# Attention and gated FFT convolution on one core: turns of q, k and x as two 64-row products, and the global keys at the end of each key tile

## The chip, the core and the metric

The kernel runs on one NeuronCore of a Trainium2 chip. The metric is the device time of one execution in microseconds (us); the median of several runs counts, and single runs of this kernel differ by some tenths of a per cent. A profile is one execution taken by the hardware profiler; its span is a little shorter than the device time. Engine names in the profile: PE is TensorE's products, PEld its weight loads, DVE is VectorE, ACT is ScalarE, POOL is GpSimd, SP is SyncE, which here only starts transfers. L711 is line 711 of the kernel.

## The reference

Causal attention with a window of 96 keys, 8 global keys and a linear bias by distance (4 batches, 8 heads, 768 positions, 64 per head), then a gated convolution over the sequence done by FFT.

```python
scores = scale * np.matmul(q, k.transpose(0, 1, 3, 2))
is_global = pos[None, :] < int(n_global)                 # 8
is_local = (rel >= 0) & (rel < int(n_local))             # 96
dist = np.where(is_global & ~is_local, float(n_local), np.abs(rel))
scores = scores - slopes[:, None, None] * dist           # kept keys only
a = softmax(scores);  x = (a @ v), heads side by side     # (4, 768, 512)
proj = x @ w_proj;  x1, x2, x3 = three parts of 512
x2_conv = irfft(rfft(x2) * rfft(filter_fft))              # length 768
out = (x1 * x2_conv * x3) @ w_out
```

## The kernel before, in words

**One list of operations, one order.** `graph()` creates some thousand operations (an operation is a few instructions on one engine), each with what it reads and writes. The string `ORDER` at the top lists their numbers, in the order in which they were created, as `357P0`: number, engine (P TensorE, V VectorE, A ScalarE, G POOL, S SP) and, for TensorE, the PSUM banks that it takes. Each engine runs its operations in that order; an instruction that waits holds up all that stand behind it on its engine. `i17b0` is 17 products on zeros at the start. The costs beside the operations served to find the order and have no effect on the chip.

**Attention** (`attention`, once per batch, in three column groups `GRP` of 2, 2 and 3 key tiles). Keys are cut into 7 tiles of 112 (`KL`); the last one starts at 656, so that it also holds 112. A tile of keys has 128 rows: rows 0 to 7 hold the 8 global keys, rows 8 to 15 zeros, rows 16 to 127 the 112 keys. Each stage:

- Loads. POOL starts one transfer per tile of q, k and v (`load_q`, `load_rows`, `load_run`). The global rows of v are copied inside SBUF by SP (`load_global`) for batches 1 to 3. In batch 0 they come by a transfer of their own into X (`first_rows`), and VectorE spreads them over the tiles. VectorE zeroes the 16 free rows of kn (named kz).
- Turns. `turned` (L661) turns q and k to put the head dimension on the partitions: per tile four 128x128 transposes as products with a unit matrix (L668), into one bank, for one tile or two; then one copy per bank by VectorE or ScalarE into QT or KT (helper line L306). For the first four tiles, `turned32` does it from float32. In groups 1 and 2 of batch 3, `crossed` has SP transpose by DMA instead. `global_keys` copies the global columns into all tiles of KT.
- Scores. `scores`: two heads side by side, each a product of 64 rows (L711), in two banks. In batch 0 the bias is added there by products (L698); in later batches exp(bias) is multiplied in afterwards. ScalarE takes the exp (L739), VectorE multiplies with the mask (L751).
- Values (`values`): 65-column products (L769, L774), a reciprocal (L799) and a scaling into xn (L793). They read the v tiles and their global rows.
- `transpose_x` (L804): turns xn into xT as `turned` does (L815), with one copy per bank.
- `gate`: products of 384 columns with parts of w (L860), x1, x3 and their product.

**Convolution** (`conv`): the sequence is folded (`butterfly`), projected (L934), transformed (L622), multiplied with the filter's transform, transformed back (L959, L962), joined, gated and projected (L986), then stored.

**Set-up.** `distances` builds the bias tables dg, near, edge and far on POOL and VectorE; `masks` takes their exp and `spread` completes it; `tables` makes the sine tables, for which ScalarE has to load another function table than for exp. The operation `warm` on ScalarE takes an exp of one number to have a table loaded early.

The change touches `ORDER`, `load_rows`, `load_first32`, `load_v`, `load_global`, `setup`, `distances`, `masks`, `turned32`, `global_keys`, `crossed`, `turned`, `scores`, `transpose_x`, `first_tiles`, `load_first` and `first_rows`; in `butterfly`, `gate` and `crossed_x` only the names of what is read and written.

Of the kernel before, what the change touches and what calls it, by code (L numbers as in the profile page):

```python
# [16 lines left out]
P = 128  # L17
NG = 8
KL = 112
LO = P - KL  # L20
HUGE = 1.0e5
# [19 lines left out]
4V 0S 1A 2S 3A 30V 9G 32A 31A 14V 13V 11V 10A 33V 22G 34V 23V 60A 62A 12V 27V 5V 65A 36G 39G 19S 35A 15V 25V 24G 63A  # L41
16V 40G 18V 42G 41G 59A 45G 28V 8V 26V 46G 48G 29A 47G i17b0 74P0 75V 61A 70P1 72P2 71V 68P3 69V 84P45 64A 106P0 76P1
37G 58A 92P67 73A 79A 78A 93P 88P23 77V 94P 85P 38G 108P1 89P 49G 86P 107A 66V 90P 95A 44G 43G 109V 112P0 113V 87A
110P1 111V 80P67 81P 82P 20V 91A 51G 67V 120P01 83A 114P45 121A 152P2 153V 50G 154P3 155V 118P67 158P0 115A 159V 119A
156P2 157V 17V 116P45 21V 117A 160P67 161A 162P23 163A 96P45 97V 98V 101P01 166P67 167A 164P45 122P23 52G 102V 103V
123V 127P01 104P6 124V 128V 53G 129V 7G 217P7 165A 105A 99P4 168P23 125P6 130P5 258G 100V 218A 126A 212P4 131A 173P01
137P5 132P6 169V 170V 171P2 213A 219V 220V 221A 174V 175V 176P7 138P3 259G 172A 357P0 214V 215V 133P2 134A 267G 266G
216A 224P6 177V 199V 198V 206V 139V 385P7 184P4 358A 55G 135V 255G 189P5 140A 141V 386V 179P7 225A 257G 355P3 256G
264G 226A 183P0 265G 359A 6A 353P1 191A 201V 143P5 227V 181A 136V 194P7 56G 57G 185A 200V 202V 356V 383P0 228V 229A
205V 260G 186A 354V 208V 230A 223V 361P23 145A 203V 196A 367P45 362A 364P67 384V 178P1 207V 148P0 365A 295P2 204V 360V  # L50
368A 180V 396P45 150A 296A 397A 390P67 209V 210V 211V 187V 363V 370P01 371A 391A 293P3 294A 270G 369V 291P2 280P0 366V
387P67 222V 292A 398V 388A 231V 232V 233V 234V 393P45 299P3 300A 394A 54G 281A 282P2 283A 429P1 273G 306P3 307A 278P6
279A 147P7 149A 286P2 372V 261S 235V 236V 272G 287A 389V 142P3 433P6 434A 271G 431P7 144A 263G 430A 485G 237V 373P45
262S 151V 268G 297P2 298A 240P6 484G 241A 182V 193P3 195A 374V 432V 238P2 239A 392V 243P6 244A 269G 375V 395V 378P01
486G 379V 380V 435P45 436A 487G 197V 438P23 439A 404P67 405V 146V 376P0 496G 406V 245P1 246A 377V 437V 581P4 284P5
285A 444P23 445A 441P67 442A 407P1 188P0 488G 582V 399P45 381P2 408A 440V 585P3 274G 190V 400V 401V 446V 583P0 382A
586V 252P67 254A 253A 275G 276G 495G 584V 402P1 403A 447P45 489G 490S 443V 613P7 614A 248P23 448V 494G 587A 249A 304P6
305A 452P01 410P7 250A 412A 500G 247V 712G 449V 450P2 453V 454V 425P6 451A 251V 501G 455P3 659P7 456V 502G 427A 493G
302V 660A 595P01 589P45 498G 478V 590A 596A 592P23 593A 588A 414P6 458P7 499G 727G 468P4 416A 301V 661P5 308V 711G
460A 303V 242V 729G 594V 409P0 657P1 658V 611P2 309V 288V 612A 289V 424P6 426A 428V 477V 479V 290V 411A 470A 662A  # L60
473P1 475A 420P7 422A 415P6 413V 312P4 480V 313A 320P5 725G 417A 324P1 472P0 321V 474A 669P23 325A 598P67 599A 523P4
481V 714G 510P1 670A 316P5 314P0 192V 511A 600V 672P23 621P67 317V 524A 715G 482V 812P1 315A 591V 673A 322P4 323A 622A
310P0 311A 813V 730G 814A 418V 419P5 318P1 319A 597V 506P4 507A 421V 491S 463P5 465A 624P67 618P01 619A 666P23 457P4
667A 519P5 674V 625A 483V 508P0 663P23 881S 615P67 713G 326V 327V 328V 329V 623V 330V 520A 664A 462P1 423V 509A 620V
720G 728G 497G 616A 521P5 492G 606P23 505G 333V 334V 464A 467P0 469A 522A 607V 601P67 466V 277G 602V 608V 459A 626V
350P1 810P5 514P0 665V 351A 716G 347P4 603A 503G 835S 671V 525P1 526A 348A 476V 344P2 717S 722G 811V 837S 504G 527P5
345A 515A 528A 617V 668V 632P67 331V 604P4 605A 678P23 532P0 633V 634V 533A 679V 512P5 513A 680V 332V 808P1 627P67
628V 882S 534P0 675P45 676V 609P2 809A 629V 535A 610A 635P1 335P3 677V 630P2 631V 529V 636A 721G 836S 471V 336A 724G
530V 883S 821P01 822A 818P67 819A 820V 815P45 816A 726G 880S 723G 838S 516V 338P3 839V 652P2 654A 681S 339A 642P6 644A
817V 648P7 531V 846P45 517V 682S 840P23 683S 650A 847A 518V 823V 824P01 825A 826V 647P6 841A 643P7 645A 638P4 640A  # L70
719G 827P01 828V 884V 341P5 829V 342A 649A 646V 653P7 849P01 850A 536V 732G 537V 461V 651V 705V 891P45 343S 892A
888P23 704V 851V 637P6 544P0 689P1 707V 639A 655A 545A 548P4 731G 691A 549A 550P6 542P5 893V 842V 540P7 543A 706V 352S
538P0 539A 552P1 553A 695P4 551A 641V 700P0 541A 702A 708V 697A 690P1 830P67 546P0 692A 848V 685P4 684P1 831V 832V
889A 687A 843P23 693V 890V 709V 885P67 340S 547A 844A 894P45 733P0 895A 886A 554V 710V 896V 718S 750P2 855P45 856V
# [1174 lines left out]
```

## Time and profile before

| | us |
|---|---|
| three runs | 170.34, 170.29, 169.12 |
| median | 170.29 |
| profiled execution, device time | 168.69 |
| its span | 166.8 |
| busy: PE, DVE, ACT, POOL | 160.3, 152.9, 144.9, 73.6 |
| first product of work (L635) to the first gate (L860) | 7.52 to 25.56 |
| last product ends | 160.7 |

The page's second part shows the span in 40 slices, a digit is a busy share in tenths:

```profile
PE   7999999999999999999999989999999999999990
DVE  5898979999999999999999979999999999999950
ACT  4589979999999998999999998999896788696731
DMA  5999999999999999999999990804052104300685
```

Three engines are busy nearly throughout, and the DMA engines up to 95 us. "Busy" counts an instruction from its start to its modelled end, and consecutive instructions overlap, so a row's mean duration is longer than the distance at which such instructions follow each other. That distance is read from start times.

### The profile page before, as it was taken

Reading aid. Unit: us, or ns where it says so; the run is one execution under the profiler, and the core shown is the slowest. Engines: PE = TensorE matmul, PEld = TensorE weight load, DVE = VectorE, ACT = ScalarE, POOL = GpSimd, SP = SyncE. Lnnn points to the kernel's source line nnn. Section 1 sums busy time; section 2 is a strip of 40 time slices with the busy share of each in tenths; the row PEclk is TensorE's granted clock in tenths of the full one; section 3 lists DMA queues with packets and bytes.
Section 4 is the critical chain, followed back from the end, with each engine's and each line's share of the span. In section 5 each row is a group of like instructions: output and inputs, shape, how many; then the busy total and the mean of one; then the engine's idle time right before and its main releaser. Section 6 shows DMA issues by size and latency. Waiting matters only on the chain.

```text
span 166.8 us, 4251 instructions
## 1 busy us (share of the span) xinstructions
PE 160.3 (96%) x1621; PEld 99.8 (60%) x1621; DVE 152.9 (92%) x336; ACT 144.9 (87%) x302; POOL 73.6 (44%) x99
## 2 busy tenths in 40 slices
PE   7999999999999999999999989999999999999990
PEld 2566787664567876666457746765744844575430
DVE  5898979999999999999999979999999999999950
ACT  4589979999999998999999998999896788696731
POOL 7999999973889934999570000000000000000000
PEclk9999999999999999999999999999999999999999
DMA  5999999999999999999999990804052104300685
GB/s 121 193 141 127 130 171 166 169 208 181 169 164 154 155 150 63 92 140 149 158 157 130 125 130 19 265 5 118 17 132 51 63 4 181 137 0 0 246 317 194
DMA packets 92916, 22.06 MB, mean 132 GB/s; under 512 B 85760, under 2 KB 89824, under 8 KB 92896
## 3 DMA queue, kind: packets, MB, share of 16 engines
q0 software_dynamic: 75952, 11.95, 100.9%
q1 hardware_dynamic: 14864, 9.33, 23.9%
q10 hardware_dynamic: 2080, 0.52, 1.7%
q8 instruction: 12, 0.20, 0.5%
q14 instruction: 8, 0.07, 0.1%
HBM read 24.94 MB, written 6.29 MB: 187 GB/s over the span
## 4 chain that ended last, share of the span: by engine, by line
PE 58%; DVE 33%; issue 4%; DMA 3%; ACT 0%; DVEq 0%; SPq 0%
PE bank L860 15%; PE bank L986 9%; DVE E L751 8%; PE bank L934 6%; PE bank L959 4%; PE bank L302 4%; DVE xn L793 4%; PE bank L698 3%; DMA KT<-kn 3%; PE bank L711 3%; PE bank L668 3%; PE bank L622 3%; PE bank L769 2%; DVE g L871 2%; PE bank L774 2%
## 5 line engine op out<-in xcount | busy, mean ns | idle before, releaser
L860 PE MATMUL bank<-xT,w 128*128 128x384 f16 x256 | 47.9, 326 | 0.0
L739 ACT ACTIVATE E<-bank 128x832 f16<-128x832 f32 (+2 forms) x64 | 42.8, 759 | 1.1 <-PE bank L711 1.0
L860 PEld LDWEIGHTS <-w 128*128 128x128 f16 x256 | 23.6, 98 | 15.4 <-issue 0.7
L322 POOL DMA_DIRECT2D kn<-in_k_dram x27 | 22.5, 848 | 6.7 <-PE bank L668 4.8
L322 POOL DMA_DIRECT2D vn<-in_v_dram x28 | 24.0, 865 | 2.2 <-DMA w<-in_moe_w_proj_dram 0.9
L986 PE MATMUL bank<-wo,y 128*128 128x512 f16 x96 | 22.9, 379 | 0.1
L751 DVE TENSOR_TENSOR E<-E,mask 128x832 f16<-128x832 f16 (+1 forms) x36 | 21.7, 622 | 0.0
L322 POOL DMA_DIRECT2D qn<-in_q_dram x21 | 18.8, 904 | 3.5 <-PE bank L934 3.2
L310 ACT ACTIVATE ot<-bank 128x512 f32<-128x512 f32 x22 | 12.8, 615 | 5.9 <-PE bank L986 3.8
L793 DVE TENSOR_TENSOR xn<-bank,rc 128x512 f16<-128x512 f32 (+1 forms) x22 | 16.8, 766 | 0.6 <-DVE rc L799 0.2
L310 ACT ACTIVATE ab<-bank 128x512 f16<-128x512 f32 x24 | 14.6, 655 | 1.2 <-PE bank L934 1.2
L869 ACT CAST g<-bank 128x384 f16<-128x384 f32 x30 | 14.5, 523 | 1.2 <-PE bank L860 1.2
L769 PEld LDWEIGHTS <-E 128*128 128x128 f16 x224 | 14.0, 97 | 2.3 <-issue 0.4
L769 PE MATMUL bank<-vn,E 128*128 128x65 f16 x224 | 15.3, 193 | 0.0
L310 ACT ACTIVATE x<-bank 128x384 f16<-128x384 f32 x26 | 13.5, 528 | 2.0 <-PE bank L860 1.3
L986 PEld LDWEIGHTS <-y 128*128 128x128 f16 x96 | 9.1, 98 | 10.1 <-DVE y L1066 0.2
L774 PE MATMUL bank<-vn,E 128*128 128x65 f16 x192 | 15.1, 193 | 0.0
L711 PE MATMUL bank<-QT,KT 64*128 64x208 f16 (+1 forms) x224 | 14.0, 244 | 0.9 <-DVE KT L306 0.7
L306 ACT CAST X<-bank 128x512 f16<-128x512 f32 x24 | 14.2, 643 | 0.3 <-PE bank L622 0.2
L306 ACT CAST eo<-bank 128x384 f16<-128x384 f32 x29 | 13.4, 542 | 0.3 <-PE bank L962 0.3
L774 PEld LDWEIGHTS <-E 128*128 128x128 f16 x192 | 13.2, 97 | 0.5
L711 PEld LDWEIGHTS <-KT 64*128 64x128 f16 x224 | 8.7, 94 | 6.4 <-issue 2.5
(148 smaller groups left out, 337.4 us busy)
## 6 DMA issues: line engine op xcount, KB each, us to landing
out_dram<-ot SPq DMA_DIRECT2D x24, 256.0 KB, 2.4
vn<-in_v_dram POOLq DMA_DIRECT2D x28, 112.0 KB, 5.4
kn<-in_k_dram POOLq DMA_DIRECT2D x27, 112.0 KB, 5.2
qn<-in_q_dram POOLq DMA_DIRECT2D x21, 128.0 KB, 5.6
w<-in_moe_w_proj_dram POOLq DMA_DIRECT2D x4, 256.0 KB, 5.7
g<-in_moe_filter_fft_dram POOLq DMA_DIRECT2D x1, 768.0 KB, 10.2
ot<-in_q_dram ACTq DMA_DIRECT2D x2, 256.0 KB, 6.6
w<-in_moe_w_proj_dram POOLq DMA_DIRECT2D x1, 512.0 KB, 7.2
```

The lines of the kernel that those rows point to most:

```text
L306: {"A": nc.scalar.copy, "V": nc.vector.tensor_copy, "G": nc.gpsimd.tensor_copy}[e](out, in_)
L310: self.nc.scalar.mul(out, in_, c)
L322: return self.g.op(eng, 0.57 + 0.00035 * nbytes[0] if eng == "G" else 0.5, lambda _: e.dma_start(dst, src), w=w, r=r, nbytes=nbytes, name= ...
L711: nc.tensor.matmul(bs[hh].f32()[:, off:off + w], self.KT[hs, hp, P * m:P * m + P], self.QT[hs, hp, KL * m:KL * m + w], start=(off == 0 and ...
L739: nc.scalar.activation(dst, src(), Act.Exp, scale=self.scale)
L751: g.op("V", dve(w, 2), lambda _: nc.vector.tensor_mul(eo, eo, mk), r=[("mask", 2 * hp), ("mask", 2 * hp + 1)], w=[("E", hp, gi)], name="ma ...
L769: nc.tensor.matmul(o[:, n, hh], ef[:, at:at + P], vt[:, t, 2 * hp + hh, 0:D + 1], start=first, stop=(t == 0), skip_group_check=True)
L774: nc.tensor.matmul(o[:, n, hh], ef[:, at:at + P], vt[:, t - 1, 2 * hp + hh, 0:D + 1], start=False, stop=True, skip_group_check=True)
L793: nc.vector.tensor_mul(to, o[:, :, :, 0:D].rearrange("p i (t h) d -> p i t h d", h=2), rc.rearrange("p i (t h) o -> p i t h o", h=2).to_br ...
L860: nc.tensor.matmul(bk.f32()[:, 0:h], self.w[:, c, o + P * j:o + P * j + P], self.xT[:, c, h * s:h * s + h], start=(c == 0), stop=(c == 3))
L869: first = g.op("AV", {"A": act(h), "V": 0.0005}, lambda e: nc.scalar.copy(x3, pts[1].f32()[:, 0:h]) if e == "A" else None, use=[pts[1]], w ...
L986: nc.tensor.matmul(bk.f32(), y[:, c, P * t:P * t + P], self.wo[:, c, :], start=(c == 0), stop=(c == 3))
```

## The change

The key tile's rows are moved: the keys stand in rows 0 to 111 (the last tile now starts at 672 and holds 96), the global keys in rows 112 to 119, and the rest is zero in KT. kn needs no zeroed rows. Every turn becomes two products: rows 0 to 63, and rows 64 to the end, on the two halves of the array, each 64 columns or less, into two banks; each bank is copied out by an operation of its own (in group 2 of `transpose_x` by two instructions). In batch 0 the global rows of v come by `load_global` as in the other batches. The tables of `distances` are built for the new rows, with instructions on rows 96 to 127 that change the rows from 112 on. `warm` takes a sine. `ORDER` is new as a whole (1,060 entries instead of 1,018), with 13 products on zeros.

```diff
-4V 0S 1A 2S 3A 30V 9G 32A 31A 14V 13V 11V 10A 33V 22G 34V 23V 60A 62A 12V 27V 5V 65A 36G 39G 19S 35A 15V 25V 24G 63A
...
+4V 0S 1A 2S 3A 16G 9G 27V 28V 29A 30V 17G 12V 20G 18V 19V 23A 33G 41G 24V 38G 7G 40G 25V 39G 8V 22A 21V 32V 58A 57A
+14V 10V i13b0 73P0 67P1 44G 31V 46G 45G 47G 34G 35S 42G 37G 43G 36S 71P2 64A 59A 49G 13V 61A 48G 60A 68A 50G 72A 69P3
...
-        self.K0 = [KL * t for t in range(6)] + [S - KL]
+        self.K0 = [KL * t for t in range(7)]
+        self.KW = [min(KL, S - x) for x in self.K0]
...
     def load_rows(self, what, dst, src, b, t):
-        lo, hi = self.K0[t], self.K0[t] + KL
-        self.load("G", dst[P - (hi - lo):P, t, :, 0:self.D],
+        lo, hi = self.K0[t], self.K0[t] + self.KW[t]
+        self.load("G", dst[0:hi - lo, t, :, 0:self.D],
...
     def load_global(self, vt, s, ng):
         for c, (t, n) in enumerate(((0, 2), (2, 5))):
-            self.load("S", vt[0:ng, t:t + n], vt[LO:LO + ng, 0:1].to_broadcast(
+            self.load("S", vt[KL:KL + ng, t:t + n], vt[0:ng, 0:1].to_broadcast(
...
-        g.op("A", 0.2, lambda _: nc.scalar.activation(self.warm, self.warm, Act.Exp),
-             r=["warm"], w=["warm"], table="exp", bias=-4000, after=self.asked)
+        g.op("A", 0.2, lambda _: nc.scalar.activation(self.warm, self.warm, Act.Sin),
+             r=["warm"], w=["warm"], table="sin", bias=-4000, after=self.asked)
...
-        g.op("V", dve(512), lambda _: v.memset(self.ot[3][0:LO], 0.0), w=["kz32"], name="kz")
-        for lo, hi in ((0, 2), (2, 7)):
-            g.op("V", dve(512 * (hi - lo), 2), lambda _, lo=lo, hi=hi: v.memset(self.kn[0:LO, lo:hi], 0.0),
-                 w=[("kz", t) for t in range(lo, hi)], name="kz")
...
     def masks(self):
-            g.op("A", act(n + self.LAST), lambda _, h=h: nc.scalar.activation(
-                mask[:, h, 2 * m:], self.dg, Act.Exp, scale=self.slopes[h]), r=["dg"],
+            g.op("A", act(n) + 0.04, lambda _, h=h: nc.scalar.activation(
+                mask[:, h, 2 * m:2 * m + n], self.dg, Act.Exp, scale=self.slopes[h]), r=["dg"],
...
+                v.tensor_copy(mask[:, hs, 2 * m + n:], mask[:, hs, 2 * m:2 * m + self.LAST])
...
-                for h in range(hs.start, hs.stop):
-                    v.tensor_scalar(mask[0:NG, h, 0:n], self.far, math.exp(-NL * self.slopes[h]), None, op0=Alu.mult)
+                v.tensor_mul(mask[96:P, hs, 0:KL], mask[96:P, hs, 0:KL], self.far[96:P, None, :].to_broadcast([32, 4, KL]))
...
     def turned(self, what, ts, buf):
-        b = g.bank()
+        bs, m = [g.bank(), g.bank()], self.KW[ts[-1]] if what == "k" else P
+        cuts = ((0, 64), (64, m))
         def turn(_):
             for x, t in enumerate(ts):
                 for i in range(4):
-                    nc.tensor.transpose(b.f16()[:, 512 * x + P * i:512 * x + P * i + P],
-                                        buf[:, t, 2 * i:2 * i + 2, :], self.ident)
+                    for bk, (lo, hi) in zip(bs, cuts):
+                        o = 64 * (n * i + x)
+                        nc.tensor.transpose(bk.f16()[:, o:o + hi - lo], buf[lo:hi, t, 2 * i:2 * i + 2, :],
+                                            self.ident[lo:hi, lo:hi])
...
+        for y, (bk, (lo, hi)) in enumerate(zip(bs, cuts)):
+            w = hi - lo
...
+            g.op("AV", {"A": act(4 * n * w), "V": dve(4 * n * w, 2, True)}, move, use=[bk],
+                 w=[(what.upper() + "T", t, y) for t in ts], name=what + "T")
...
     def transpose_x(self, j, c):
-                    nc.tensor.transpose(tx[:, o:o + P], self.xn[:, t, 2 * j + i], self.ident)
+                    for y, bk in enumerate(bs):
+                        o, lo, hi = 64 * (nt * i + n), 64 * y, ws[n] if y else 64
+                        nc.tensor.transpose(bk.f16()[:, o:o + hi - lo], self.xn[lo:hi, t, 2 * j + i],
+                                            self.ident[lo:hi, lo:hi])
...
     def load_first(self):
-        self.first_rows(vt)
...
-                self.load_run(("vn", 0), vt, self.v, t, 1)
+                self.load_rows(("vn", 0), vt, self.v, 0, t)
+                if t == 0:
+                    self.load_global(vt, 0, LO)
```

## The prediction

> **What bounds the kernel now.** I read first the table of stages (busy time of every engine in chosen stretches), because the shares of the page are means over the whole span.
>
> ```profile
> core 0: us, PE busy (x) PEld busy (x) DVE busy (x) ACT busy (x) POOL busy (x), PEclk, DMA share, GB/s
> 8.00:25.00 17.00, 17.00 (x292) 12.43 (x289) 14.63 (x43) 14.94 (x29) 17.00 (x22) 1.00 1.97 142
> 25.00:36.00 11.00, 10.96 (x127) 7.90 (x125) 10.66 (x27) 10.65 (x22) 10.45 (x13) 1.00 1.93 177
> 64.00:80.00 16.00, 16.00 (x148) 10.29 (x147) 15.90 (x32) 15.46 (x34) 14.20 (x18) 1.00 1.68 121
> 99.00:112.00 13.00, 13.00 (x138) 8.80 (x134) 12.89 (x27) 12.30 (x27) 0.00 (x0) 1.00 0.43 95
> ```
>
> From 25 us on, TensorE and VectorE are both full and ScalarE nearly. A busy TensorE need not be one at its pace, so I counted columns: a 384-column product starts every 162 ns (four in 0.65 us), a 128-column turn every 55 ns, pairs of 64 rows count half. That gives 15.6 us of work in 64 to 80, 12.8 in 99 to 112, and about 133 us from 25 to 160.7 us, where the last product ends (a stretch of 135.7). TensorE is the bound after 25 us, with VectorE close behind: its idle time in the same stretch sums to 4.5 us. Before 25 us ScalarE sets the pace: the twelve blocks of exps run almost without a gap from 11.63 to 22.3 us. The chain that ended last says the same of the middle from the other side; from 36 to 93 us it runs through VectorE alone, one instruction behind the other:
>
> ```profile
> 49.09 0.50 DVE E L751
> 49.58 0.60 DVE xn L793
> 50.19 0.46 DVE E L751
> ```
>
> Then I read the start times of TensorE's instructions, which price the two things that the change does to it.
>
> ```profile
> 17.26 0.20 PE L698 MATMUL bank<-dg,eo 64*128 64x96 bf16 x1
> ...
> 17.48 0.20 PE L698 MATMUL bank<-eo 64*128 64x96 bf16 x1
> 17.50 0.20 PE L698 MATMUL bank<-dg,eo 64*128 64x96 bf16 x1
> 17.52 0.40 PE L711 MATMUL bank<-QT,KT 64*128 64x208 f16 x6
> ```
> ```profile
> 52.33 0.61 PE L668 MATMUL bank<-ident,qn 128*128 128x128 f16 x8
> 52.77 0.59 PE L622 MATMUL bank<-ab,fwd 128*128 128x512 f16 x2
> 53.30 0.62 PE L711 MATMUL bank<-QT,KT 64*128 64x208 f16 x12
> 53.85 0.40 PE L815 MATMUL bank<-ident,xn 128*128 128x128 f16 x4
> ```
>
> Two 96-column products of 64 rows, on different halves of the array, start 20 ns apart and the next starts 20 ns later: 40 ns a pair. Eight full turns take 0.44 us (52.33 to 52.77). Two 512-column products should take 0.43 us, yet the scores after them start after 0.53: entering 64-row work costs 0.10 us, and so it does at 61.83, 103.38 and 111.77. Leaving it costs 0.02 (twelve scores are six pairs of 87 ns, 0.52 of the 0.55 us to 53.85) up to 0.12 (four scores at 62.53, the next product at 62.82, 0.29 for 0.17).
>
> The rows that price the evacuations and the one new wait:
>
> ```profile
> L306 DVE COPY QT<-bank 128x512 f16<-128x512 f16 x6 | 2.5, 415 | 0.0
> L306 DVE COPY QT<-bank 128x1024 f16<-128x1024 f16 x3 | 2.1, 686 | 0.1
> L306 DVE COPY vn<-vn 16x2560 f16<-16x2560 f16 x1 | 1.4, 1416 | 0.0
> L396 DVE MEMSET kn<- 16x1280 uint32 x1 | 1.1, 1125 | 0.2 <-issue 0.2
> ```
> ```profile
> vn<-vn SPq DMA_DIRECT2D x1, 48.0 KB, 5.6
> ```
>
> **The change part by part.** The time is the sum's base: the profiled execution took 168.69 us (span 166.8 and 1.9 around it), the three runs 169.12, 170.29 and 170.34. The middle of the four is 169.7, and the sum is added to that.
>
> *Shorter turns.* 232 turns (88 of k, 72 of q, 72 of x) become pairs of 64 columns. The pair costs at least 27 ns (64/208 of 89 ns) and at most the 40 ns of the 96-column pair; I take 34, halfway, so 21 ns less than 55 (15 to 28). 180 of them lie after the first gate product, where TensorE bounds: -3.8 us (-2.7 to -5.0). The other 52 lie where exps pace: 0.
>
> *More switches.* I went through both orders and marked each TensorE operation as 64-row (scores, biases, and after the change turns) or 128-row. Entries into 64-row work rise from 21 to 36, all 15 in the part between the first gate product and the last turn; the new order puts the remaining turns beside scores or each other. At 0.12 to 0.22 us for in and out, take 0.17: +2.55 us (+1.8 to +3.3). The Trainium skill, "TensorEngine Tiling (Array Packing)", section Key Properties, says that changing the tiling mode drains TensorE; the trace agrees with the 0.10 us at 53.30. The page has no price; without that rule the sum would be 2.55 us lower. TensorE together: -1.25 us (-3.2 to +0.6).
>
> *More evacuations.* 24 copies on VectorE and 20 on ScalarE become 58 and 38, with about the same elements. Consecutive VectorE copies start 0.33 us apart for 512 and 0.60 for 1024 (at 66.50 and 34.20), so each extra one costs 0.07 us. After the first gate VectorE has +2.5 us of them; two eo, two ab, one ot and one x3 come over from ScalarE (+3.0 at 0.47, 0.60, 0.61 and 0.27); one spread of the masks moves behind that point (+1.1); five x1 leave (-2.35 at 0.47), the range reduction of the sines moves ahead of it (-2.0: 0.59, 0.42, 0.42 and 0.69, overlapped), and small table copies leave (-0.7). Net +1.6 us on an engine with 4.5 us idle there: 0 on the path, up to +1.6 if its idle times don't fall where the copies come.
>
> *Set-up.* The memsets of kn (1.12 and 0.48) and ot (0.48), the two copies into vn (0.67 and 1.42), and the 0.60 us row edge go; marks, short masks and the row product replace them at less. All lie before 25 us, where VectorE sits idle 2.4 us and the exps pace: 0. ScalarE loads tables three times (2.09, 25.49, 31.12; 1.28 us each); the new order still alternates exp, sin, exp, but puts the sin load right behind the last exp, where ScalarE waited 0.86 us for a turn. ScalarE isn't the last in any stage after 25 us: 0, at best -1.3. Four busy products fewer end TensorE's warming 0.86 us earlier, but the second and third q tile land 6.6 us after their issue at 0.74 to 2.0: 0, at best -0.8. Tile 6 of k and v loads 96 rows instead of 112, 1,024 packets less of 92,916: 0.
>
> *The v copy.* Before, the first 16 rows of v came by a transfer of their own at 1.88 us and were spread by VectorE. Now two SP transfers inside SBUF copy them, and they wait for v tile 0, which POOL issues at 11.8 (12.1 with the longer far table ahead) and which landed 5.3 us later: 17.4. Such a copy took 5.6 us at 40.7, while loads of the same moment took 7.4; loads at 15 to 17 us took 3.9, and a transfer of an idle queue 2.4. So the first values product starts at 20 to 23, I take 21.5 (loads then were half as slow), against 18.51. Behind the waiting product stand in TensorE's queue one block of scores, hence the last exp, and all values and turns of x. From the first values to the first gate the new order needs 0.36 for the product, four times 0.85 for reciprocal and scaling, a turn and its copies: 4.4 us. That puts the first gate at 25.9 against 25.56: +0.3 us (-1.2 to +1.8).
>
> Sum: -1.25 + 0.3 = -0.95, so **168.8 us**. Both ends added: -5 and +4.
>
> **The rivals.**
> *All of the saving arrives (0.18).* Pairs at 27 ns, switches at 0.12, the v copy hidden, the start a little earlier: -3 to -4, about 166.2. For it: TensorE is the fullest engine, so what it sheds should show. Against: with +1.6 us of work in 3 us less of time, VectorE's idle time after 25 us would have to go from 4.5 us to none.
> *VectorE becomes the bound, slower (0.20).* From 36 to 93 us the chain that ended last already runs through VectorE almost alone, and its queue is in order: a half copy that waits holds up the masks and scalings behind it. Its +2.5 and +3.0 us come in that stretch, while the -2.0 and part of the -2.35 lie elsewhere. It decides once the extra exceeds the idle time there (0.8 us from 36 to 93 in the table of stages); then nothing of TensorE's gain is left and +2 to +4 comes in: about 172.5.
> *The v copy takes 5.6 us or more (0.10).* First gate at 27.4 to 28.5, TensorE's gain kept: +0.6 to +2.5, about 171.2. ScalarE and VectorE idle with it, so nothing catches up.
> *No side by side (0.07).* If each half turn keeps the 30 ns that 65-column products of 128 rows take (L769 and L774 start 30 ns apart), the pair costs 60: 180 x 5 ns and 15 x 0.22 give +4.2, 173.9. The 40 ns pair speaks against. The Trainium skill, "TensorE: Matmul & The Clock Gate", section "Wait — 56ns, not 53.3ns?", states a floor of about 25 ns from start to start; per instruction that would make 50 ns a pair, 0.9 us saved against 2.55 of switches, 171.3. The 20 ns above disagree where the two are on different halves.
>
> **The numbers.** About 1% (1.7 us, so under 168.6 or over 172.0) is what a measurement of this kernel tells from no change; its own runs spread by 0.7%. The forecast has 0.45, its own range 167.3 to 170.4, half of it on each side of 168.6. Faster: 0.22 + 0.17 = 0.39. Same: 0.22 of the forecast, 0.01, 0.08 of the VectorE case and 0.05 of the v copy, 0.36. Slower: 0.01, 0.12, 0.05 and 0.07: 0.25. The range 165.6 to 172.6 leaves out the far end of each.
>
> **What would show it.** Right: turns as 64-row pairs starting 27 to 40 ns apart; 0.10 us lost ahead of turns that follow 128-row work; TensorE without gaps after 26 us; first values product at 20 to 23 us, released by a vn copy. Wrong: pairs at 50 ns or more; VectorE without idle time while TensorE has gaps; a first gate after 27 us, or before 25; a gap at the b3 scores (93 to 99 us) that is longer than today's 0.7 us.

## The result and the profile after

The changed kernel takes 174.71 us (median of four runs, 173.94 to 177.58), the kernel before 170.23 on the same chip: a ratio of 1.028 with an interval of 1.021 to 1.034, so by the ratio 4.7 us slower (3.6 to 5.8). The forecast was 168.8, with a range of 165.6 to 172.6. The ratios here and below leave out executions that took over 1.5% longer than the fastest of the same kernel; the profiles of e1, e2, e6 and e13 are of such ones (granted clock 0.50 for 3 to 14 us), so sums over the whole of them are rough.

The profiled execution took 173.94 us with a span of 172.2. First its slices, to be laid beside those of before:

```profile
PE   7688999999999999999999899999999999999990
DVE  2779679999989999999999699999999999999950
ACT  3549899999889989899999799999995889866851
...
PEclk9999999999999999999999999999999999999998
```

The clock was full throughout, so nothing of the 5.4 us of longer span is a throttle's. TensorE's row is thinner in the second to fourth slice, from 4 to 17 us. The table of stages (busy time of each engine in a stretch, number of instructions in brackets) says more:

```profile
core 0: us, PE busy (x) PEld busy (x) DVE busy (x) ACT busy (x) POOL busy (x), PEclk, DMA share, GB/s
8.00:25.00 17.00, 14.83 (x276) 11.05 (x277) 13.10 (x47) 13.08 (x23) 17.00 (x22) 1.00 1.99 144
25.00:36.00 11.00, 10.55 (x199) 7.29 (x196) 10.66 (x29) 10.67 (x25) 8.63 (x11) 1.00 1.91 178
64.00:80.00 16.00, 15.90 (x163) 8.72 (x156) 15.25 (x35) 15.31 (x32) 11.61 (x14) 1.00 1.46 98
99.00:112.00 13.00, 13.00 (x108) 7.71 (x109) 12.86 (x24) 12.80 (x26) 0.00 (x0) 1.00 0.29 95
```

From 8 to 25 us TensorE was busy 17.00 before and is 14.83 now; VectorE and ScalarE lost 1.5 and 1.9 us (14.63 to 13.10, 14.94 to 13.08). Nobody took the time over: all three stand idle for longer. The first gate product starts at 28.51 us instead of 25.39, and the last product ends at 168.12 instead of 162.50 (both by the records of TensorE; the 25.56 and 160.7 given for before are a little off from these). So 3.1 us of the 5.6 are there at the first gate, the others come behind it. What TensorE waits for (line that waits, who released it, total us, times, longest), first all that stands behind the warming products in the kernel before, then the changed kernel:

```profile
PE bank L711 <- DVE KT L306: 0.7, 1, 0.7
PE bank L711 <- DVE xT L306: 0.2, 1, 0.2
```
```profile
PE bank L635 <- DVE p L311: 2.1, 1, 2.1
...
PE bank L714 <- DMA QT<-qn: 0.9, 2, 0.7
PE bank L772 <- DVE xn L796: 0.6, 2, 0.3
PE bank L670 <- DVE y L416: 0.4, 1, 0.4
```

The first turn waits 2.1 us for the float32 unit matrix p, a table copy that the new order puts behind thirteen other VectorE operations. The scores of batch 3 wait for the transfer of q. Adding up all gaps above 0.15 us between TensorE's instructions from the last warming product on (start times, each instruction's end taken at its own column count), I get 1.6 us before and 7.2 after: the difference is as long as the loss. TensorE's column work shrank at the same time, by some 7 us (142.6 to 135.7, two halves side by side counted as one), but the gaps below 0.15 us, in which the changes between products of different row counts lie, grew by about as much (10.7 to 18.2 between the first product of work and the last). What it shed in columns it spent again on these.

The turns themselves, by TensorE's start times (start, duration, operation, shape, count):

```profile
41.02 0.41 PE L670 MATMUL bank<-ident,kn 64*128 64x64 f16 x16
41.24 0.42 PE L670 MATMUL bank<-ident,qn 64*128 64x64 f16 x16
```
```profile
71.50 1.07 PE L670 MATMUL bank<-ident,kn 64*128 64x64 f16 x8
72.50 0.35 PE L714 MATMUL bank<-QT,KT 64*128 64x208 f16 x4
72.69 0.40 PE L670 MATMUL bank<-ident,kn 64*128 64x64 f16 x16
73.01 0.82 PE L874 MATMUL bank<-xT,w 128*128 128x384 f16 x4
```

Sixteen half products, eight pairs, start 0.22 us before the next turn (41.02 to 41.24): 27.5 ns a pair, side by side. Ahead of a gate, which has 128 rows, the same eight pairs take 0.32 (72.69 to 73.01): leaving the 64-row work costs 0.10. But the turn at 71.50, with four pairs, takes 1.00 us instead of 0.11. It is tile 6 of k, which holds 96 keys: its upper product has 32 rows, and the group's label shows only its lower half's shape.

The chain that ended last runs less through VectorE than it did (shares of the span, first before, then after):

```profile
PE 58%; DVE 33%; issue 4%; DMA 3%; ACT 0%; DVEq 0%; SPq 0%
```
```profile
PE 66%; DVE 18%; ACT 6%; DMA 4%; issue 3%; ACTq 1%; DVEq 0%
```

Two of VectorE's rows show what the doubled copies cost (busy us, mean ns): a copy of half the columns takes 283 ns, not half of 420. The last row is the copy of the global rows of v inside SBUF, 5.1 us from issue to landing:

```profile
L311 DVE COPY QT<-bank 128x256 f16<-128x256 f16 x10 | 2.7, 283 | 0.0
...
L311 DVE COPY QT<-bank 128x512 f16<-128x512 f16 x6 | 2.4, 420 | 0.0
```
```profile
vn<-vn SPq DMA_DIRECT2D x2, 48.0 KB, 5.1
```

### The profile page after: what moved, and what is told of

Read it like the earlier page. It is cut to its first block, busy times and chain, and to the rows that moved or that the text cites. A ratio compares the mean times of both kernels' runs of the same rounds, so it can differ in the third digit from the quotient of the medians.

```text
span 172.2 us, 4792 instructions
## 1 busy us (share of the span) xinstructions
PE 161.7 (94%) x1849; PEld 96.6 (56%) x1849; DVE 153.1 (89%) x364; ACT 146.8 (85%) x319; POOL 72.4 (42%) x99
## 4 chain that ended last, share of the span: by engine, by line
PE 66%; DVE 18%; ACT 6%; DMA 4%; issue 3%; ACTq 1%; DVEq 0%
PE bank L874 16%; PE bank L1000 12%; PE bank L948 11%; PE bank L973 5%; PE bank L622 4%; PE bank L714 4%; DMA QT<-qn 4%; PE bank L670 3%; DVE xn L796 3%; ACT E L742 3%; DVE E L754 3%; PE bank L772 2%; PE bank L777 2%; PE bank L701 2%; PE bank L818 1%
## 5 line engine op out<-in xcount | busy, mean ns | idle before, releaser
L742 ACT ACTIVATE E<-bank 128x832 f16<-128x832 f32 (+2 forms) x64 | 43.7, 758 | 3.5 <-PE bank L714 2.9
L327 POOL DMA_DIRECT2D vn<-in_v_dram x28 | 23.2, 848 | 4.2 <-DMA g<-in_moe_filter_fft_dram 3.2
L754 DVE TENSOR_TENSOR E<-E,mask 128x832 f16<-128x832 f16 (+1 forms) x36 | 21.5, 617 | 0.0
L327 POOL DMA_DIRECT2D qn<-in_q_dram x21 | 19.3, 923 | 4.1 <-PE bank L714 2.9
L315 ACT ACTIVATE x<-bank 128x384 f16<-128x384 f32 x31 | 16.0, 532 | 1.8 <-PE bank L874 1.8
L714 PE MATMUL bank<-QT,KT 64*128 64x208 f16 (+1 forms) x224 | 15.7, 244 | 1.2 <-DMA QT<-qn 0.9
L315 ACT ACTIVATE ab<-bank 128x512 f16<-128x512 f32 x22 | 13.2, 655 | 0.7 <-PE bank L948 0.7
L311 ACT CAST eo<-bank 128x384 f16<-128x384 f32 x27 | 12.2, 513 | 0.9 <-PE bank L976 0.8
```

Of the source, the lines that this page charges most:

```text
L311: {"A": nc.scalar.copy, "V": nc.vector.tensor_copy, "G": nc.gpsimd.tensor_copy}[e](out, in_)
L315: self.nc.scalar.mul(out, in_, c)
L327: return self.g.op(eng, 0.57 + 0.00035 * nbytes[0] if eng == "G" else 0.5, lambda _: e.dma_start(dst, src), w=w, r=r, nbytes=nbytes, name= ...
L714: nc.tensor.matmul(bs[hh].f32()[:, off:off + w], self.KT[hs, hp, P * m:P * m + P], self.QT[hs, hp, KL * m:KL * m + w], start=(off == 0 and ...
L742: nc.scalar.activation(dst, src(), Act.Exp, scale=self.scale)
L754: g.op("V", dve(w, 2), lambda _: nc.vector.tensor_mul(eo, eo, mk), r=[("mask", 2 * hp), ("mask", 2 * hp + 1)], w=[("E", hp, gi)], name="ma ...
```

## The experiments

All kernels were timed beside the kernel before on the same chip; the ratio to it is what compares them. "After" stands for the changed kernel. None beats the kernel before.

| run | what it is | ratio | interval |
|---|---|---|---|
| after | | 1.0278 | 1.0214 to 1.0342 |
| e1 | after, no 32-row products | 1.0162 | 1.0118 to 1.0206 |
| e2 | after, unit matrix early | 1.0262 | 1.0209 to 1.0315 |
| e3 | e1 and e2 | 1.0196 | 1.0143 to 1.0249 |
| e5 | e3, 17 warming products | 1.0283 | 1.0185 to 1.0380 |
| e6 | e5, rows of v early | 1.0215 | 1.0142 to 1.0288 |
| e9 | e6, sine behind x | 1.0241 | 1.0150 to 1.0331 |
| e11 | e9, crossed scores later | 1.0345 | 1.0298 to 1.0391 |
| e15 | e9, angles late, values early | 1.0487 | 1.0409 to 1.0564 |
| e7 | e6, full turns, two banks, two copies | 1.0291 | 1.0247 to 1.0335 |
| e13 | e7, one bank, one copy | 1.0240 | 1.0188 to 1.0292 |
| e8 | before, two copies for one | 1.0101 | 1.0053 to 1.0149 |
| e12 | before, split turns in the old order | 1.0831 | 1.0795 to 1.0868 |

**e1: the pieces of 32 rows.** Rows 96 to 127 of tile 6 are zeroed, and its upper product has 48 rows like the others (for x, 48 rows of which 32 are copied).

```diff
+        rows = ((0, 64), (64, KL if what == "k" else P))
...
-                    for bk, (lo, hi) in zip(bs, cuts):
+                    for bk, (lo, hi) in zip(bs, rows):
...
-                        o, lo, hi = 64 * (nt * i + n), 64 * y, ws[n] if y else 64
+                        o, lo, hi = 64 * (nt * i + n), 64 * y, KL if y else 64
```

> The changed kernel with one edit: the upper product of tile 6 takes 48 rows (rows 96 to 111 of kn zeroed once) instead of 32; what is copied out stays the same, so no part of the result changes. Theory A (products of 32 rows switch the array's mode within a turn; in the changed profile four pairs of tile 6 of k take 0.90 us against 0.16 for four ordinary pairs, and six pairs of x with tile 6 0.61 against 0.25): 20 such products at 0.18 us, 3.7 us of TensorE, those before the first gate partly hidden: 2 to 3.5 us faster than the changed kernel's 174.3, about 171.5, and the turns of tile 6 take 0.2 us. Theory B (the late start of the first turn is the loss): under 0.5 us, about 174. Theory C (VectorE is the bound through the added copies): under 0.7 us, gaps on TensorE grow by what the turns shed.

The same turn of k, and one of x that took 0.61 us in after (63.01 to 63.62), by TensorE's start times in e1:

```profile
72.74 0.29 PE L671 MATMUL bank<-ident,kn 64*128 64x64 f16 x8
72.86 0.35 PE L715 MATMUL bank<-QT,KT 64*128 64x208 f16 x4
```
```profile
64.54 0.34 PE L819 MATMUL bank<-ident,xn 64*128 64x64 f16 x12 [0.15 <-DVE xT L311]
64.83 0.39 PE L671 MATMUL bank<-ident,kn 64*128 64x64 f16 x16
```

The turn of k falls from 1.00 to 0.12 us, that of x from 0.61 to 0.29. There are three such turns of k and four of x, so 3.9 us of TensorE's time (3 x 0.88 + 4 x 0.32). The time falls by 1.2% of 170, 2.0 us (0.7 to 3.3 by the two intervals, which don't overlap). So the 32-row pieces are 2.0 of the 4.7 us. The Trainium skill, "TensorEngine Tiling (Array Packing)", section Key Properties, says that a change of tiling mode drains TensorE; these rows agree and give the price, eight changes for 0.88 us, 0.11 each.

**e2, e3, e5, e6: the start.** e2 moves the unit matrix (10V) from behind thirteen VectorE operations to behind the third; e3 is e2 with e1's edit; e5 puts back the 17 warming products; e6 moves the load of v tile 0 (34G) and SP's two copies of its global rows forward.

```diff
-... 27V 28V 29A 30V ... 14V 10V i13b0 ...
+... 27V 28V 10V 29A 30V ... 14V i13b0 ...
```
```diff
-14V i13b0 73P0
+14V i17b0 73P0
```
```diff
-... 40G 25V 39G 8V ... 14V i17b0 ... 47G 34G 35S 42G 37G 43G 36S 71P2
+... 40G 25V 39G 34G 8V ... 14V 35S 36S i17b0 ... 47G 42G 37G 43G 71P2
```

> The changed kernel with one entry of the order moved: the float32 copy of the unit matrix (10V) goes from behind the ones (VectorE's 14th operation, at 8.84 us) to behind the first slope (at about 1.9 us). Theory B: the first turn starts at about 7.0 instead of 9.12 us, right behind the warming; the first gate and the end come 1.5 to 2 us earlier: about 172.5. If the v copy takes over as what the first values wait for (it landed at about 21.6, they start at 21.96), only 0.4 us of it arrives: about 174. Theories A and C alone: no more than that 0.4.

> Both edits of the two runs before. If A and B are both right and their losses lie one behind the other: the sum of the two gains, 4 to 5 us, 169.5 to 170, as fast as the kernel before or a little faster. If the v copy or VectorE takes over: less than the sum by 1.5 us or more, about 171.5 to 172.

> The run with both edits, and 17 products on zeros instead of 13. Theory D (TensorE's granted clock drops to 0.50 for 3 to 5 us when it has stood idle for 2 us or more in 3.4, as at 12 to 16 us of the run with both edits and after the gap at 96 us of others): no gap ahead of the first turn, clock 1.00 up to 90 us, and runs that lie closer together; 0.5 to 1.5 us faster than the run with both edits, about 171. If the clock is not decided by these gaps: the same 172, with the drop still at 12 to 16 us.

> The run before, and the load of v tile 0 moved ahead of the last four loads of q and k in POOL's order (the two SP copies with it). Theory E (the copies of the global rows of v hold the first values products, which in the runs with an early start waited 0.6 to 1.0 us for vn<-vn): the copies land before 19 us, the wait is gone, the first gate comes 0.6 to 2 us earlier (26.5 to 27.8 against 28.4), 170 to 170.5. If the exps and the order of the scores ahead of them hold the first values: first values at 21 us still, under 0.4 us gained.

The largest single wait of after goes, and next to nothing comes of it: 1.0262 for 1.0278. What TensorE waits for in e2:

```profile
PE bank L714 <- DMA QT<-qn: 1.8, 1, 1.8
PE bank L635 <- DMA ot<-in_k_dram: 1.3, 1, 1.3
...
PE bank L772 <- DMA vn<-vn: 1.0, 1, 1.0
PE bank L772 <- DVE xn L796: 0.9, 2, 0.5
```

The first turn now starts at 7.21 us instead of 9.12, held by a load, and the first values wait 1.0 us for the copy of v's rows, so the first gate starts at 28.29 instead of 28.51. With both edits (e3) the ratio is 1.0196, no better than e1's alone (1.0162). With the 17 warming products (e5) the clock is full from 6.6 us to the end of the work, as theory D had it, but the first values wait 1.6 us for the copy of v's rows and the time is not lower (1.0283, overlapping e3's). With the rows of v early as well (e6) the first gate starts at 27.69, still 2.3 us later than before, and the ratio is 1.0215, which e1 and e3 overlap: theory E's gain of 2 us doesn't come. The start's waits are real, but where one goes the next one shows.

**e9: sines behind x.** In the new order the load of the sine table, 1.28 us on ScalarE, stands between the last exp and the copies of x.

```diff
-... 128P45 275S 6A 103V 99P67 ... 188V 235A
+... 128P45 275S 103V 99P67 ... 188V 6A 235A
```

> The kernel of e6 with one edit: the first use of the sine on ScalarE, which brings the sin table in, stands behind the copies of x of the first projections instead of ahead of them. Theory F (in the new order the table's load of 1.28 us stands on ScalarE between the last exponential and the copies that the first gate needs): in the profile the first gate starts 0.9 to 1.3 us earlier than in e6 (27.69), at 26.4 to 26.8, and the fastest time falls from 171.2 to 170.0 to 170.5. Rival (the copies of x are not what the first gate waits for, the values are, or TensorE's own queue): the first gate stays within 0.4 us of 27.69 and the time within 0.5 us.

ScalarE's instructions in e9 (start, us, operation, count, idle before):

```profile
23.93 0.68 ACT L311 COPY xT<-bank 128x256 f16<-128x256 f16 x2
25.08 0.37 ACT L311 COPY xT<-bank 128x256 f16<-128x256 f16 x1 [0.47 <-PE bank L819]
26.39 0.32 ACT L311 COPY xT<-bank 128x192 f16<-128x192 f16 x1 [0.94 <-PE bank L819]
26.73 1.28 ACT L373 ACT_TABLE_LOAD   x1
```

The copies start 1.5 us earlier than in e6 (25.46), and then wait for TensorE's turns of x. The first gate is at 27.78 (27.69 in e6), the time the same within the intervals: theory F falls.

**e14, e15: angles late, values early.** e14 takes the products of angles and their copies from ahead of the first scores to ahead of the sines. e15 also puts the first values behind two of the scores of the third group instead of three.

```diff
-... 231P1 ... 232A ... 226P2 ... 233V 234V ... 227A 228V 229V ... 188V 6A 235A
+... 188V 231P2 226P3 232A 233V 234V 227A 228V 229V 6A 235A
```
```diff
-178P01 179A 172P23 173A 65V 176P67 177A 15V 96P45 97V 98V 174P01 175A 102P23
+15V 178P01 179A 172P23 173A 96P45 97V 98V 65V 176P67 177A 102P23 103V 104V 174P01 175A
```

> The kernel of e9 with one edit of the order: the two products of angles, their two copies on ScalarE and their four instructions on VectorE stand right ahead of the sines, behind the copies of x, instead of ahead of the first scores. Theory A (2.0 us of VectorE and 1.0 us of ScalarE for the angles stand between the first turns and the first exponentials, and the copies of q and k that the first scores need come behind them): the first exponential starts 0.4 to 1.0 us earlier than in e9 (11.93), the last of the first batch's ends as much earlier, TensorE's idle time from 10 to 30 us falls below 1.5 us (2.7 in e9), and the fastest time is 171.0 to 172.0 beside 172.6. Rival (the work has to be done all the same ahead of the first gates, which the sines' chain then holds): the time stays within 0.5 us or rises.

> The kernel of e14 with one more edit of the order: the first product with the values stands behind two of the four scores of the third group instead of behind three, as in the kernel before, and the next one ahead of the last score. Theory L (VectorE's chain of reciprocal and scaling, 0.9 us for each of the first batch's values, starts late because TensorE reaches the first values late): the first values start 0.6 us or more earlier than in e14, the first gate 0.4 us or more earlier, and the time falls by as much. Rival (the last exponential sets the first gate): the values start earlier and the first gate and the time stay within 0.3 us.

e14 gives little: its runs spread from 176.2 to 182.8, and in the profiled one, 548 us, TensorE's 384-column products took 883 ns on average instead of 326, for which nothing in the trace gives a reason. e15 is clearly slower, 1.0487. Its values start at 20.75 us (21.30 in e9), its first gate at 29.02 (27.78). TensorE's waits in e15:

```profile
PE bank L667 <- DMA kn<-in_k_dram: 1.8, 1, 1.8
PE bank L667 <- DVE y L412: 1.5, 1, 1.5
PE bank L711 <- DMA QT<-qn: 1.4, 1, 1.4
```

Without the angles TensorE runs up against the loads of k (at 16.5 us), and batch 1's first turn (from 29.8 to 31.39) waits for a bank that VectorE's late work on the angles still reads. The first exponential starts at 11.93 in e15 as in e9, so theory A's sign doesn't come, and the first gate is later, so theory L falls.

**e11: the crossed scores of batch 3.** Four products of other stages are put ahead of the scores that wait for the transfer of q.

```diff
-883P01 544V 504V 886P67 ... 933P23 ... 560P5 ... 349P4 690P0 ... 684P5 ... 685P6
+544V 504V ... 560P5 561A 349P4 350A 684P5 686A 685P6 687A 933P23 934A 883P01 884A 885V 886P67
```

> The kernel of e9 with one more edit: in batch 3 four products of other stages (a product forward, an output, two gates) and the score that waits for nothing are put ahead of the first scores of the crossed tiles, which waited 1.60 us for the transfer QT<-qn in e9. Theory Q (the new order asks for the crossed q some 1 to 3 us before its transfer lands): the wait is below 0.8 us, no granted clock below 0.9 between 90 and 105 us, and the time is 0.5 to 2.0 us under e9's fastest 172.6. Rival (the work that filled the gap is missing later, since VectorE and ScalarE set the pace of this stage): the wait goes, and the time stays within 0.5 us of e9.

The wait for QT<-qn, 1.60 us in e9, is gone; now a gate further on waits 1.39 us for the exps that had been put off:

```profile
PE bank L876 <- ACT E L744: 1.4, 1, 1.4
...
PE bank L716 <- DVE rc L804: 0.9, 1, 0.9
```

The time is not lower (1.0345 beside 1.0241, with intervals that overlap a little). Theory Q falls, and the wait comes back as the rival had it, if anything with a loss: in this stage the scores feed ScalarE and VectorE.

**e4, e7, e13: the new order without the split.** e4 is after with full turns of 128, 112 or (tile 6) 96 rows into the same two banks (two pairs of heads in each), with two copies; e7 is the same in the kernel of e6. e13 puts e7's turns back into one bank with one copy; the places of all other instructions stay, and the one copy stands where the first of the two stood.

```diff
-                    for bk, (lo, hi) in zip(bs, cuts):
-                        o = 64 * (n * i + x)
-                        nc.tensor.transpose(bk.f16()[:, o:o + hi - lo], buf[lo:hi, t, 2 * i:2 * i + 2, :],
-                                            self.ident[lo:hi, lo:hi])
...
+                    o = P * (n * (i % 2) + x)
+                    nc.tensor.transpose(bs[i // 2].f16()[:, o:o + m], buf[0:m, t, 2 * i:2 * i + 2, :],
+                                        self.ident[0:m, 0:m])
```
```diff
-                    o = P * (n * (i % 2) + x)
-                    nc.tensor.transpose(bs[i // 2].f16()[:, o:o + m], ...
+                    o = P * (n * i + x)
+                    nc.tensor.transpose(bs[0].f16()[:, o:o + m], ...
...
+                if y:
+                    return
```

> The changed kernel with every turn as one full product of 128 or 112 rows again, in the new order and layout, still into two banks (one for the first two head pairs, one for the other two; for x one per slice) and still two copies each, of the same number of elements. It takes away the 64-row and 32-row modes of the turns and nothing else (and the second instruction of the x copies of the last group, 8 instructions). Theory A with the switches: the turns cost 232 x 55 ns = 12.8 us, against 212 x 40 ns, 20 x 0.22 us and 15 more entries of 0.1 to 0.2 us, 15 us: about 2 us faster than the changed kernel, 172. Theory C: the copies bind, so less work on TensorE changes nothing: 174 within 0.7. If side by side is worth what the 40 ns a pair say and only tile 6 is wrong, this run is slower than the 48-row run by up to 1 us.

> The run before with every turn as one full product (as in the earlier run with full turns). It tells in a kernel without the late start and without 32-row products what side by side is worth: if the 40 ns a pair less the switches count, 232 x 15 ns less 15 x 0.15 us: 1 us slower than the run before, about 171.3; if the switches eat it: the same within 0.4; if VectorE and the copies bind: the same within 0.4 too, with TensorE's gaps smaller.

> The kernel of e7 (the new order and set-up, mended at its start, with full turns of 128 or 112 rows into two banks and two copies) with each turn put back into one bank with one copy, as before the change; the order, its edits of the set-up, and the places of all other instructions stay. Theory N (what is left is the new order and set-up): the time stays within 1 us of e7's 173.4 to 173.9, so at 172.5 to 174, with TensorE idle 5 us or more in all. Rival B (what is left is the second bank and the second copy that the turns need, as the 18 us of idle TensorE in e12 suggest): 169 to 171, with TensorE idle under 4 us.

e4's fastest, the only one of its times to set beside others, is 174.34, e1's are 171.21 to 172.26. e7 took 173.4 to 173.9, e6 with its split turns 171.2 to 173.3; their intervals overlap a little. So beside full turns into two banks, split ones without 32-row pieces may gain some 1 to 3 us in the new order. e13 is the telling one: with each turn as one product into one bank with one copy, as before the change, but in the new order and set-up, it still takes 1.024 (1.019 to 1.029), 4.1 us more than before. TensorE's waits in e13:

```profile
PE bank L713 <- DMA QT<-qn: 1.6, 2, 1.3
...
PE bank L713 <- DVE QT L311: 0.6, 1, 0.6
PE bank L713 <- DVE KT L311: 0.3, 1, 0.3
PE bank L771 <- DVE xn L795: 0.3, 1, 0.3
```

By the count of gaps TensorE idles 6.1 us in it (7.0 in e7, 1.6 before), spread over 10 to 40, 50 to 70 and 90 to 100 us. Theory N holds, rival B falls: going back to one bank and one copy doesn't bring the time back.

One reservation belongs to e13: the new order was made for half copies, and the whole copies, up to 686 ns on VectorE (1024 columns) where a half takes 420, now stand in the place of the first half. Part of its 4.1 us can be this misfit, and no run separates it. But ahead of the first gate the loss doesn't depend on how the turns are made. In the profiles whose clock was full up to there (after, e2, e5, e6 and e11 with split turns, e7 with full ones) the first gate starts at 27.50 to 28.51 us, 2.1 to 3.1 later than before. From the first gate to the end of the last product it takes 137.1 us before, 139.6 in after, 138.5 in e5 and 139.5 in e7, one profile each: once the 32-row pieces are gone, split turns lose 1.3 us there and full ones 2.4.

**e8, e12: the old order.** e8 makes two instructions of every copy of a turn, 52 more; e12 splits 31 of the 44 f16 turns of the kernel before, wherever its order leaves a second bank free, with 64-row pieces only.

```diff
-            self.copy(e, *((dst[:, 0], src[:, 0]) if n == 1 else (dst, src)))
+            for c0, c1 in ((0, 64), (64, P - lo)):
+                d, s = dst[:, :, :, c0:c1], src[:, :, :, c0:c1]
+                self.copy(e, *((d[:, 0], s[:, 0]) if n == 1 else (d, s)))
```
```diff
+                    if b2.users:
+                        for bk, r in ((b, 0), (b2, 64)):
+                            at = 256 * x + 64 * i
+                            nc.tensor.transpose(bk.f16()[:, at:at + 64], buf[r:r + 64, t, 2 * i:2 * i + 2, :],
+                                                self.ident[r:r + 64, r:r + 64])
+                        continue
```

> The kernel before, with each copy of a turn made as two instructions of half the columns on the same engine (four for x in the last group): 52 instructions more, and nothing else. Theory C: at 0.07 us each on engines that are full from 25 to 93 us, 52 of them (24 copies of VectorE become some 31 more instructions with those of the x group) cost 2 us or more: 171 or more. If their idle time takes them in: under 0.7 us, 169.1 to 169.8.

> The kernel before in its own order, its key tiles and set-up untouched, with 31 of its 44 turns of f16 tiles split into two products of 64 rows side by side wherever the order has a second bank free for as long; both banks are copied by the instruction's own engine, one copy behind the other, and none of the pieces has 32 rows. Theory O (the split itself is about even, and the loss of the change is the new order and the set-up that goes with it): 168.5 to 170.5, at most 1.5 us above before, idle TensorE below 3 us in all. Rival S (the split loses by itself, by mode changes and twice the copies): 172 or more, with TensorE idle or waiting for copies in the stages of the turns.

The copies cost 1.0%, 1.7 us (0.9 to 2.5), between the two forecasts. e12 is the slowest of the table, 183.25 us, 14 us above before. Theory O falls; rival S has the side (172 or more), but from changes of mode and copies it gives no such size. TensorE's waits:

```profile
PE bank L868 <- ACT E L790: 2.3, 2, 1.2
PE bank L708 <- DVE QT L341: 1.6, 2, 1.0
```

And one of these turns by its start times:

```profile
56.49 0.20 PE L868 MATMUL bank<-ident,xn 64*128 64x64 f16 x1
57.90 0.27 PE L868 MATMUL bank<-ident,xn 64*128 64x64 f16 x7 [1.21 <-ACT E L790]
```

The first half product runs at 56.49; its partner, into the second bank, runs at 57.90, when ScalarE's exp is done, which has nothing to do with x. I take it that the exp was still reading scores from that bank. Idle TensorE sums to 18.2 us, 16.6 more than before, and the time is up by 14. The Trainium skill, "TensorEngine Tiling (Array Packing)", section Gotcha 1: PSUM Pressure, says that row tiles have to write to different PSUM banks, which raises the pressure on them. The run shows how much that can be: the old order had a bank free by its own list, but not by the clock. Split in this way, the old order doesn't hold its time; whether another choice of banks, or copies on two engines, would, no run tests.

## Why the prediction was wrong

**The step that failed** is "Set-up", with the order taken along in it: it named the edits and priced their instructions, found that "all lie before 25 us, where VectorE sits idle 2.4 us and the exps pace: 0", and put no price on the order itself. The new order was marked for one thing only, its entries into 64-row work. So the first gate was put 0.3 us later and came 3.1 later (28.51 for 25.39), past the 27 us that the prediction itself named as a sign of being wrong. e13 measures order and set-up without the split: +4.1 us (3.2 to 5.0), with the reservation made there. The idle time that should have covered the set-up didn't: the new order has waits there on VectorE's tables, on loads, and on v's rows, one behind another. Why the same stretch held in the old order is not shown, and no run separates the order from the set-up.

**Which place of the order makes it, stays open.** The unit matrix, the warming products, v's rows, the sine load, the crossed scores, the angles and the first values were each moved. Moved alone or in these combinations, none gave a time that could be told from the one it started from, save the angles and the first values together (e15), which made it worse (the angles were not measured cleanly by themselves).

**The turns** came out better than put: 27.5 ns a pair, the lower end of 27 to 40. **The switches** cost 0.10 to get out (72.69 to 73.01), and to get in 0.10 as I had read. That is 0.20 for both, inside 0.12 to 0.22. The low end, 0.02 to get out, was a misreading: of the six pairs at 53.30 two have 96 columns, which the group's label hides, so 0.11 of the 0.55 us is the exit. By these the TensorE term would be a saving of 180 x 27.5 ns = 4.95 less 15 x 0.20 = 3.0, a gain of 2.0 us where I put 1.25. Its kind was right, but it left out the next item, 3.9 us of TensorE's time, which turns it into a loss.

**The 32-row pieces** were missed, though the diff showed the last tile with 96 keys and my own text had a price for changes between 64-row and 128-row products: I applied it between operations and not within one. +2.0 us by e1. This is the second step that failed.

**The copies** at "0, up to +1.6": e8 gives +1.7 (0.9 to 2.5) in the old order, where they lie on VectorE and ScalarE with little to spare. There the zero was too kind. In the new one e7 and e13 can't be told apart.

**The v copy** was right in its first half: the first values start at 21.96, within 20 to 23, near the 21.5 taken. From there to the first gate I added 4.4 us and it took 6.55, so 28.51 instead of 25.9. The kernel before needs 6.88 for the same stretch (18.51 to 25.39): I took the new order to be 2.5 us faster there, and it is not. But the copy is not the cause of the late gate by itself: e6, with the copy earlier, starts it only 0.5 us before e5 (28.21).

**The rivals.** "VectorE becomes the bound" has the sign and nearly the size (172.5), yet not the mechanism: e13 has one copy a turn and is as slow, and the chain through VectorE got shorter. "No side by side" is refuted by the 27.5 ns. "The v copy late" gives the late gate for a reason that e6 takes away. The case that happened, a new order in which all three engines stand idle for longer, was not among them.

**The sum afterwards:** order and set-up +4.1 (e13), 32-row pieces +2.0 (e1), together 6.1 of which 4.7 are left; so by difference the split with its copies and banks gives back 1.4. Directly, e13 beside e6 shows 0.4 us, with intervals that overlap; that it gives back anything at all, beyond its own copies, is not shown.

## What to carry to other kernels

When a change brings a new order by hand, price the order as a step of its own: list for each engine what each early instruction now stands behind, and give the range a side for new waits even if all added work fits into idle time. Splitting a product into row halves takes a second PSUM bank, as it did here, for as long as the copy lasts; look by start and end times, not by the list, whether there is one, and keep the pieces' row counts close (here 48 rows ran beside 64 without a loss, 32 did not). Where several waits stand in a row, taking the largest away tells only what the next one is.

## What the runs showed of the hardware

**A change between 64-row and 32-row products inside one turn costs about 0.11 us each time.** In after the turn of tile 6 took 1.00 us for four pairs of 64 and 32 rows, in e1 0.12 for four pairs of 64 and 48; the eight single products in after start 0.12 to 0.13 us apart.

**The granted clock can fall in short idle stretches and stay low behind them.** In the profiled execution of e6 TensorE waited 2.74 us for QT<-qn up to 96 us; windows of 4 us (the column behind POOL is the granted clock):

```profile
88.00:92.00 4.00, 4.00 (x60) 2.51 (x58) 4.00 (x9) 4.00 (x11) 0.00 (x0) 1.00 2.04 146
92.00:96.00 4.00, 0.35 (x9) 0.14 (x4) 2.05 (x5) 0.38 (x1) 0.00 (x0) 0.92 1.56 100
96.00:100.00 4.00, 4.00 (x31) 1.60 (x31) 0.55 (x3) 2.64 (x5) 0.00 (x0) 0.66 0.69 137
100.00:104.00 4.00, 4.00 (x34) 2.13 (x33) 3.97 (x10) 4.00 (x9) 0.00 (x0) 1.00 0.01 2
```

It went the same way in e1 behind 3.0 us at 9 us (0.56 from 8 to 12, 0.50 from 12 to 16) and in e15 in a wait of 1.5 us that ended at 31.39 (0.85 from 28 to 32, 0.50 from 32 to 36). In after 2.1 us at 7 to 9 us had no such effect, nor had 1.5 us at 92 us in e3. The kernel before, with no gap over 0.9 us, didn't show it; but e3 did early on, from 12 to 16 us (0.61), behind gaps of 0.9 and 0.7 us. The Trainium skill, "TensorE: Matmul & The Clock Gate", section "HAM oscillation — how this bites in real kernels", puts the limit at idle gaps of some 3.4 us; in e3, e6 and e15 shorter ones were enough, so here the measurement decides. Why equal gaps differ, no run shows.
